# Decay attention and a hard-swish MLP on one core: the first batch's maxima leave by GpSimd's queue, and the MLP's last products rotate over five PSUM buffers

## The chip, the cores and the metric

The kernel runs on one core of one Trainium2 chip. The metric is the time of one execution on the device in microseconds (us). Each kernel is run several times and the median counts. TensorE (PE) multiplies matrices into PSUM, VectorE (DVE), ScalarE (ACT) and GpSimd (POOL) work element by element, and SyncE (SP) issues transfers (DMAs). Each engine runs its instructions in the order in which they were laid down at build time and waits on semaphores for what the others have not finished. GpSimd can also issue transfers, in line with its own instructions.

## The reference

Eight batches of eight heads (576 positions, 64 wide) go through attention with a learned decay; the result, 4608 rows of 512, goes through a two-layer network with a hard-swish between the layers.

```python
scores = scale * np.matmul(q, k.transpose(0, 1, 3, 2))
cum = np.cumsum(np.log(np.clip(f, 0.0001, 1.0)), axis=-1)
decay = cum[:, :, :, None] - cum[:, :, None, :]
scores = np.where(causal, -1000000000.0, scores + decay)
scores = scores - np.max(scores, axis=-1, keepdims=True)
attn = np.exp(scores)
attn = attn / (np.sum(attn, axis=-1, keepdims=True) + 1e-09)
x = np.matmul(attn, v)           # then transposed to 4608 x 512
h = x @ w_in                     # 512 x 2048
g = h * np.clip(h + 3.0, 0.0, 6.0) / 6.0
out = g @ w_out                  # 2048 x 512
```

[...]

## The kernel before, in words

**The weights.** w_in and w_out come in 16 chunks each of 512 KB (`w_load`, the DMA on L238, by SP). Each chunk is decoded (ACT L251, DVE L252 and L253), squared and summed (ACT L257); per group of four chunks of w_in, and once for the whole of w_out, a scale is worked out (`pow2_scale`, a matmul on L184 and four small DVE steps; L341 for w_out), and each chunk is split into a high and a low half of 16 bits: ACT L284 writes the high one. For the first three groups of w_in the low one goes through PE (L287, L288, tiles `low`) and ACT L289; for the last group of w_in and all 16 chunks of w_out it is one DVE instruction of 128x512 (L295). The second layer's first product (`po`, L832) can start only once w_out is split.

**The first batch's attention.** Batch 0 is worked in 12 steps, which `VH` lists: four pairs of heads on their first 256 queries (kind A), then eight heads on the rest (kind B). Each step takes the maximum per query of a first, cheaper product: `natural` (PE L495, tile `pn`, then DVE L501 into `MC`), `max_rows` (PE L510 turns the maxima into rows, tile `ptm`; DVE L512 negates them into `mr`, of which there is one buffer; a DMA on L513 puts them into row 96 of `TQ`), and then `scores` (PE L559, L560, L562 into `ps`, which reads that row; ACT L578 takes the exponential) and `av` (PE L713). POOL copies queries and keys and takes the low halves (L449, L450, L464, L469). The other 56 heads (`rows`, kind F) take another path without L513.

**The MLP.** `h_unit` makes 128 of the 2048 hidden units for 512 rows (`ph`, PE L785 to L787, then ACT L791, DVE L794, ACT L795, DVE L796), `out_unit` a 128x512 block of the output (`po`, PE L832 to L834, ACT L838, the DMA on L841). `rest_unit` (`ph_r`, L808 to L810, then ACT L817, DVE L821, ACT L823, DVE L824) and `out_unit` again (`po_r`) do the 64 odd rows of two batches together. These units are spread between the steps of attention by a count of credits (`fill`).

**PSUM.** Eight banks: pool `ps_s` has two buffers of two banks each (`pn` and `ps` of attention), `ps_m` two of one bank, `ps_t` one, and `pav` takes the last. `mm_tile` gives each unit of the MLP its PSUM tile: by turns two of three from `ps_m` and the third from `ps_t`.

**What sets the order.** The program is written in one order, but at build time a scheduler simulates it and lays down each engine's instructions in the order in which it finds them ready. Where a queue or a pool changes, its order can change on all engines. One help ties a few loads by hand: `pinned()` sets that what is issued within it comes after the instruction last put into the list `small`, and acts between instructions of one engine. The list holds the DMAs of L430 (the decay rows, by SP) and those of L513, one more with each of the 12 steps. `pinned()` holds the first eight loads of w_in (L236) and all loads of the values V (L353), both on SP.

Of the kernel before, what the change touches and what calls it, by code (L numbers as in the profile page):

```python
# [11 lines left out]
F32 = mybir.dt.float32  # L12
# [8 lines left out]
def kernel(  # L21
# [10 lines left out]
    nc = tc.nc  # L32

    NHEAD, D, S = qk.shape
# [5 lines left out]
    P = 128  # L40
# [6 lines left out]
    TT = 512  # L47
# [7 lines left out]
    ps_s = ctx.enter_context(tc.tile_pool(name="ps_s", bufs=2, space=bass.MemoryType.PSUM))  # L55
# [52 lines left out]
    TQ = [cpool.tile([97, SP], F32R, name=f"TQ{i}") for i in range(NQK)]  # L108
# [365 lines left out]
    def chunks(v):  # L474
        kind = VH[v][0]
        if kind == "A":
            c = [(h * QA + i * P, h * QA, P, (i + 1) * P, 512 * h + P * i) for h in range(2) for i in range(CA)]
            return [list(enumerate(c)), []]
        places = {3: 0, 2: 512, 4: 384}
        return [  # L480
            [(c - CA, ((c - CA) * P, 0, CR[c], c * P + CR[c], places[c])) for c in h]
            for h in ((3, 2), (4, ))
        ]
# [22 lines left out]
    def max_rows(v):  # L506
        i = v % NQK
        m = sum(len(x) for x in chunks(v))
        pt = ps_t.tile([P, 512], F32, tag="tr", name=f"ptm_{v}")
        nc.tensor.matmul(pt[:m, :P], MC[v % 2][:, 0:m], identr, start=True, stop=True)  # L510
        mr = p2.tile([NCH, P], F32R, tag="mr", name=f"mr_{v}", bufs=1)
        nc.vector.tensor_scalar(mr[:m], pt[:m, :P], -1.0, None, op0=ALU.mult)  # L512
        d = nc.sync.dma_start(TQ[i].bitcast(F32)[96:97, 0:m * P], mr.bitcast(F32)[:m])  # L513
        small.append(d.ins)


# [233 lines left out]
    def x_move(v):  # L750

        kind, n = VH[v]
        g = n if kind == "A" else n // 2
        b, cc = divmod(g, NPAIR)
        xhl = xpair[g][1]
        c0, c1, rest = {"A": (0, CA, None), "B": (CA, NCH - 1, NCH - 1), "F": (1, NCH, 0)}[kind]
        o = c0 - (1 if kind == "F" else 0)
        if rest is not None:
            nc.sync.dma_start_transpose(
                xT[2][:, cc, b // 2, :, 64 * (b % 2):64 * (b % 2) + 64],  # L760
                xhl[0:64, rest].rearrange("p a e -> p (a e)"),
            )
        nc.sync.dma_start_transpose(
            xT[b % 2][:, cc, o:o + c1 - c0].rearrange("p c a t -> p (c a) t"),
            xhl[:, c0:c1].rearrange("p c a e -> p (c a e)"),
        )


    turn = [0]

    def mm_tile(name, three):

        turn[0] += 1
        if three and turn[0] % 3 == 0:
            return ps_t.tile([P, TT], F32, tag="tr", name=name)
        return ps_m.tile([P, TT], F32, tag="mm", name=name)

    def h_unit(x, fc, c0, c1, b, three, name):

        nw = c1 - c0  # L780
        ph = mm_tile(f"ph_{name}_{fc}_{c0}", three)[:, :nw]
        fs_ = slice(fc * P, (fc + 1) * P)
        for cc in range(NCC):
            xh, xl = (x[:, cc, c0 // P:c1 // P, hl] for hl in range(2))
            nc.tensor.matmul(ph, w1[0][:, cc, fs_], xh, start=(cc == 0), stop=False)  # L785
            nc.tensor.matmul(ph, w1[0][:, cc, fs_], xl, start=False, stop=False)  # L786
            nc.tensor.matmul(ph, w1[1][:, cc, fs_], xh, start=False, stop=(cc == NCC - 1))  # L787
            if cc == 1 and nw == TT:
                yield H_COST
        r = p2.tile([P, TT], F32, tag="rt", name=f"r_{name}_{fc}_{c0}", bufs=3)[:, :nw]  # L790
        nc.scalar.activation(  # L791
            r, ph, AF.Relu, bias=bias_r, scale=scol(A1 + NG * b + fc * NG // NFC)
        )
        nc.vector.scalar_tensor_tensor(r, r, 6.0 * CG, ph, op0=ALU.min, op1=ALU.mult)  # L794
        nc.scalar.copy(gT[:, 0, fc, c0:c1], r)  # L795
        nc.vector.tensor_tensor(gT[:, 1, fc, c0:c1], r, gT[:, 0, fc, c0:c1], op=ALU.subtract)  # L796
        yield H_COST
# [47 lines left out]
    def moe_in(b, c0=0, c1=TT):  # L845

        for fc in range(NFC):
            j, new = divmod(fc, NFC // NG)
            if new == 0 and c0 == 0:
                while j not in w_in_done:  # L850
                    next(w_in_q, None)
                moe_scale_in(b, j)
            yield from h_unit(xT[b % 2], fc, c0, c1, b, b > 0 or c0 > 0, f"{b}")

    def moe_out(b, c0=0, c1=TT):

        if b == 0:
            for _ in wq:
                pass
        if c0 == 0:  # L860
            moe_scale_out(b)
        for s in range(c0 // P, c1 // P):
            r = S * b + (64 if b else 0) + s * P
            yield from out_unit(s, UO + b, [(r, r + P)], b > 0 or s * P >= QA, f"{b}")
# [4 lines left out]
    def rest_in(k, g):  # L869

        for j in range(NG):
            yield from rest_unit(k, j, g)

    def rest_out(k, g):

        b = 2 * k
        r = S - 64 if b == 0 else S * b
        yield from out_unit(
            0, UX + b + 1, [(r, r + 64), (S * (b + 1), S * (b + 1) + 64)], True, f"r{k}", g
        )  # L880
# [30 lines left out]
    for i in range(NL):  # L911
        nc.gpsimd.memset(T1[i].bitcast(F32)[:, S:], 0.0)
    max_rows(0)
    rests(0)
    load_x(2)
# [17 lines left out]
    def fill(k):  # L933
        credit[0] += k * rates[0]
        while credit[0] >= 1 and units:
            with tc.high_priority(offset=-LOW_M):
                r = next(units[0], 0)
            if r == 0:
                units.pop(0)
            else:  # L940
                credit[0] -= r
        credit[0] = min(credit[0], 1.0)

    def done(v):
        kind, n = VH[v]
        if kind == "A":
            if n == NPAIR - 1:
                units.append(moe_in(0, 0, QA))
                units.append(moe_out(0, 0, QA))
            return  # L950
        b, h = divmod(n, H)
        if h == H - 1:
            cut = QA if b == 0 else 0
            units.append(moe_in(b, cut, TT))
            if b == B - 1:
                units.append(rest_in(b // 2, g_end))
            units.append(moe_out(b, cut, TT))
            if b == B - 1:
                units.append(rest_out(b // 2, g_end))
            elif b % 2:  # L960
                units.append(rest_in(b // 2, gT))
                units.append(rest_out(b // 2, gT))

    prev = None
    pend_x = None
    vq = v_scale(0)
    for i, (kind, n) in enumerate(VH):
# [27 lines left out]
        if i + 1 < NV and VH[i + 1][0] != "F":  # L995
            max_rows(i + 1)
# [32 lines left out]
        prev = (i, ph)  # L1029
# [2 lines left out]
    fill(4)  # L1032
    x_move(prev[0])
    done(prev[0])
    while units:
        fill(1)

# [35 lines left out]
```

## Time and profile before

| | before |
|---|---|
| median of 3 runs | 1069.62 us (1068.02 to 1071.15) |
| profiled execution | 1067.75 us |
| its span, first to last instruction | 1065.7 us |
| PE busy | 1005.6 us (94%) |
| DVE busy | 714.6 us (67%) |
| ACT busy | 633.5 us (59%) |
| POOL busy | 439.4 us (41%) |
| mean granted TensorE clock | 0.988 of full speed |

The span is the time from the first to the last instruction of the profiled execution; its own time on the device is 2.05 us longer. The views give, per line of the program, how long an engine was busy, how long it idled before those instructions, and whose work ended the idling. "L295 DVE ... w<-w,SC" is line 295 on VectorE, output and inputs by the program's names. A table by stages gives each engine's busy time, and in brackets its instructions, within one stretch of the span.

### The profile page before, as it was taken

Reading aid. Unit: us, or ns where it says so; the run is one execution under the profiler, and the core shown is the slowest. Engines: PE = TensorE matmul, PEld = TensorE weight load, DVE = VectorE, ACT = ScalarE, POOL = GpSimd, SP = SyncE. Lnnn points to the kernel's source line nnn. Section 1 sums busy time; section 2 is a strip of 40 time slices with the busy share of each in tenths; the row PEclk is TensorE's granted clock in tenths of the full one; section 3 lists DMA queues with packets and bytes.
Section 4 is the critical chain, followed back from the end, with each engine's and each line's share of the span. In section 5 each row is a group of like instructions: output and inputs, shape, how many; then the busy total and the mean of one; then the engine's idle time right before and its main releaser. Section 6 shows DMA issues by size and latency. Waiting matters only on the chain.

```text
span 1065.7 us, 21332 instructions
## 1 busy us (share of the span) xinstructions
PE 1005.6 (94%) x7650; PEld 598.6 (56%) x7650; DVE 714.6 (67%) x1887; ACT 633.5 (59%) x1257; POOL 439.4 (41%) x641
## 2 busy tenths in 40 slices
PE   2799967899999999999999999999999999999897
PEld 2567844665555755555555755555555755444543
DVE  6878799886867678866885778847895677115300
ACT  5798667766864657656755657646764666125301
POOL 9635556435544445454553445545544430000000
PEclk9999989999999999999999999999999999999999
DMA  8875446936766675567565755566556544010000
GB/s 239 275 216 174 110 101 136 210 77 118 158 118 120 119 160 106 95 144 154 104 125 109 160 112 109 106 130 163 105 97 137 91 89 74 12 40 1 1 20 30
DMA packets 253717, 123.83 MB, mean 116 GB/s; under 512 B 225860, under 2 KB 227452, under 8 KB 253612
## 3 DMA queue, kind: packets, MB, share of 16 engines
q1 hardware_dynamic: 253612, 122.47, 53.2%
q8 instruction: 60, 0.98, 0.4%
q14 instruction: 45, 0.37, 0.1%
HBM read 47.93 MB, written 9.73 MB: 54 GB/s over the span
## 4 chain that ended last, share of the span: by engine, by line
PE 81%; DVE 9%; ACT 4%; DMA 4%; issue 2%; SPq 0%; POOL 0%; ACTq 0%; DVEq 0%; POOLq 0%
PE ph L785 10%; PE ph L786 10%; PE ph L787 10%; PE po L832 10%; PE po L834 10%; PE po L833 10%; PE pn L622 3%; PE pn L619 3%; DMA ring<-in_w_in_dram 2%; DVE pp L630 1%; PE pav L706 1%; PE pav L707 1%; PE pav L705 1%; PE po_r L834 1%; PE ph_r L808 1%
## 5 line engine op out<-in xcount | busy, mean ns | idle before, releaser
L642 ACT ACTIVATE pp<-pp,nb 128x192 f32<-128x192 f32 x280 | 138.4, 552 | 133.7 <-DVE nb L636 119.6
L785 PE MATMUL ph<-xT,w 128*128 128x512 f16 (+1 forms) x576 | 198.4, 358 | 3.6 <-ACT o L838 2.3
L659 DVE TENSOR_TENSOR ring<-pp,ring 128x128 f16<-128x128 f32 (+2 forms) x216 | 142.2, 671 | 83.5 <-ACT ring L656 77.8
L787 PE MATMUL ph<-xT,w 128*128 128x512 f16 (+1 forms) x576 | 197.9, 357 | 0.0
L786 PE MATMUL ph<-xT,w 128*128 128x512 f16 (+1 forms) x576 | 197.8, 357 | 0.0
L832 PE MATMUL po<-w,gT 128*128 128x512 f16 x512 | 189.5, 381 | 7.5 <-ACT w L284 3.5
L833 PE MATMUL po<-w,gT 128*128 128x512 f16 x512 | 192.1, 381 | 3.7 <-DVE w L295 3.7
L464 POOL TENSOR_TENSOR T<-ST,TQ 64x288 fp32r<-64x288 f32 (+2 forms) x136 | 112.0, 825 | 199.2 <-PE pn L622 153.0
L834 PE MATMUL po<-w,gT 128*128 128x512 f16 x512 | 191.7, 381 | 0.0
L630 DVE CUSTOM_DVE_ANT_0 pp<-pn,W 128x192 f32<-128x192 f32 x280 | 123.5, 483 | 32.1 <-PE pn L622 21.9
L794 DVE SCALAR_TENSOR_TENSOR r<-r,ph 128x512 f32<-128x512 f32 (+1 forms) x144 | 89.1, 620 | 68.1 <-ACT r L791 67.5
L619 PE MATMUL pn<-TK,TQ 68*128 68x192 f32 x336 | 125.9, 388 | 5.8 <-issue 5.7
L469 POOL TENSOR_TENSOR T<-ST,T 64x288 fp32r<-64x288 f32 (+1 forms) x136 | 125.5, 941 | 12.6 <-ACT T L462 7.9
L791 ACT ACTIVATE r<-ph,bias_r,SC 128x512 f32<-128x512 f32 (+1 forms) x144 | 103.8, 725 | 26.0 <-PE ph L787 22.8
L796 DVE TENSOR_TENSOR gT<-r,gT 128x512 f16<-128x512 f32 (+1 forms) x144 | 102.5, 714 | 23.5 <-ACT gT L795 21.8
L622 PE MATMUL pn<-T,T 128*128 128x192 f32 x336 | 116.0, 370 | 0.0
L656 ACT CAST ring<-pp 128x192 f16<-128x192 f32 x280 | 114.4, 450 | 0.2
L795 ACT CAST gT<-r 128x512 f16<-128x512 f32 (+1 forms) x144 | 81.1, 566 | 40.6 <-DVE r L794 40.2
L665 POOL TENSOR_TENSOR ring<-pp,ring 128x128 f16<-128x128 f32 x96 | 56.1, 584 | 104.0 <-ACT ring L656 84.4
L834 PEld LDWEIGHTS <-gT 128*128 128x128 f16 x560 | 54.7, 98 | 70.0 <-issue 10.3
L833 PEld LDWEIGHTS <-gT 128*128 128x128 f16 x560 | 54.9, 98 | 65.1 <-issue 10.2
L787 PEld LDWEIGHTS <-w 128*128 128x128 f16 x576 | 56.5, 98 | 57.0 <-issue 6.6
(159 smaller groups left out, 2036.3 us busy)
## 6 DMA issues: line engine op xcount, KB each, us to landing
ST<-in_qk_dram SPq DMA_DIRECT2D x64, 288.0 KB
ring<-in_w_out_dram SPq DMA_DIRECT2D x16, 512.0 KB
out_dram<-o SPq DMA_DIRECT2D x32, 256.0 KB
T<-TQ SPq DMA_DIRECT2D x56, 144.0 KB
vst<-in_vS_dram SPq DMA_DIRECT2D x7, 1040.0 KB
ring<-in_w_in_dram SPq DMA_DIRECT2D x9, 512.0 KB
w<-in_w_in_dram SPq DMA_DIRECT2D x7, 512.0 KB
vst<-in_vS_dram SPq DMA_DIRECT2D x14, 130.0 KB
```

What stands on the lines that cost most here:

```text
L469: nc.gpsimd.tensor_tensor(T1[j][0:D, a:e], s[D:, a:e], T1[j][D:, a:e].bitcast(F32), op=ALU.subtract)
L619: nc.tensor.matmul(dst, TQ[i][0:D + 4, qs], TK[i][0:D + 4, a:e], start=True, stop=False)
L622: nc.tensor.matmul(dst, T7[j][:, qs], T1[j][:, a:e], start=False, stop=True)
L630: nc.vector.tensor_tensor_reduce(pp[:r, w:w + kw], pn[:r, o:o + kw], W[:r, 4 * P + r - kw:4 * P + r], 1.0, -3.0e38, ALU.add, ALU.max, accu ...
L642: nc.scalar.activation(x_, x_, AF.Exp, bias=nb[:r, e0 + x:e0 + x + 1], scale=0.125)
L659: eng.tensor_tensor(hl[:r, a:a + c * P], pp[:r, at[c] + 64:at[c] + kw], hl[:r, h0[c] + 64:h0[c] + kw], op=ALU.subtract,)
L785: nc.tensor.matmul(ph, w1[0][:, cc, fs_], xh, start=(cc == 0), stop=False)
L786: nc.tensor.matmul(ph, w1[0][:, cc, fs_], xl, start=False, stop=False)
L787: nc.tensor.matmul(ph, w1[1][:, cc, fs_], xh, start=False, stop=(cc == NCC - 1))
L832: nc.tensor.matmul(po, g[:, 0, fc, ts_], w2[:, fc, 0, :], start=(fc == 0), stop=False)
L833: nc.tensor.matmul(po, g[:, 0, fc, ts_], w2[:, fc, 1, :], start=False, stop=False)
L834: nc.tensor.matmul(po, g[:, 1, fc, ts_], w2[:, fc, 0, :], start=False, stop=(fc == NFC - 1))
```

## The change

The DMA of L513, twelve times, is issued by POOL in place of SP. It is still put into `small`, so the list now holds POOL's instructions, and the loads in `pinned()` are on SP. After the last head's outputs have been moved, a list `heads_done` is no longer empty, and from then on `mm_tile` takes each odd turn from `ps_s`, whose two buffers attention no longer uses (512 of their 1024 columns); even turns go on as before.

```diff
@@ max_rows
         mr = p2.tile([NCH, P], F32R, tag="mr", name=f"mr_{v}", bufs=1)
         nc.vector.tensor_scalar(mr[:m], pt[:m, :P], -1.0, None, op0=ALU.mult)
-        d = nc.sync.dma_start(TQ[i].bitcast(F32)[96:97, 0:m * P], mr.bitcast(F32)[:m])
+        d = nc.gpsimd.dma_start(TQ[i].bitcast(F32)[96:97, 0:m * P], mr.bitcast(F32)[:m])
         small.append(d.ins)
@@ mm_tile
     turn = [0]
+    heads_done = []
 
     def mm_tile(name, three):
 
         turn[0] += 1
+        if heads_done and turn[0] % 2:
+            return ps_s.tile([P, 1024], F32, tag="S", name=name)[:, :TT]
         if three and turn[0] % 3 == 0:
             return ps_t.tile([P, TT], F32, tag="tr", name=name)
         return ps_m.tile([P, TT], F32, tag="mm", name=name)
@@ the end of the program
     fill(4)
     x_move(prev[0])
     done(prev[0])
+    heads_done.append(prev[0])
     while units:
         fill(1)
```

Lines below 770 stand three further down in the changed kernel (L832 becomes L835). The scheduler lays the work down in another order in two stretches: from the start up to the end of w_out's split, and after the last head. Between them, and in what is executed, nothing differs on PE, DVE and ACT. The following shows three of the places, each row an instruction with its line, its output and inputs, and their shape; the numbers in the names tell buffers apart.

SP's queue near the start, from the first rows of the decay on. `TK<-cs` are the decay rows of the first two pairs of heads, `T_101<-TQ_93` the queries' halves of the first, and `w_115`, `ring` the slots for chunks of w_in. Before:

```order
L409 DMA ST_104<-in_qk_dram 128x2x256
L409 DMA ST_105<-in_qk_dram 128x2x256
L430 DMA TK_96<-cs 2x1x256 x2
L430 DMA TK_97<-cs 2x1x256 x2
L461 DMA T_101<-TQ_93 64x512
L917 DMA decay_dram<-cs 64x1152
L238 DMA ring_125<-in_w_in_dram 128x1024
L238 DMA w_115<-in_w_in_dram 128x1024
L424 DMA TK_98<-decay_dram 2x2x256
L409 DMA ST_103<-in_qk_dram 128x2x256
L513 DMA TQ_93<-mr_186 1x4x128
L355 DMA v_111<-in_vS_dram 128x3x520
```

and in the changed kernel:

```order
L409 DMA ST_104<-in_qk_dram 128x2x256
L409 DMA ST_105<-in_qk_dram 128x2x256
L355 DMA v_111<-in_vS_dram 128x3x520
L356 DMA xT_118<-in_vS_dram 128x520
L357 DMA xT_118<-in_vS_dram 64x520
L238 DMA w_115<-in_w_in_dram 128x1024 x2
L430 DMA TK_96<-cs 2x1x256 x2
L430 DMA TK_97<-cs 2x1x256 x2
L461 DMA T_101<-TQ_93 64x512
L920 DMA decay_dram<-cs 64x1152
L238 DMA ring_123<-in_w_in_dram 128x1024
L238 DMA ring_125<-in_w_in_dram 128x1024
```

The three loads of V and two chunks of w_in have moved ahead of the first pairs' decay rows, and L513 is gone from the queue. On PE the same start has the `low` products of the first chunks of w_in ahead of the first pair's scores; in the changed kernel these rows stand just ahead of and at the first `ps`, which before follows the second `pn` at once:

```order
L288 MATMUL low_343<-w_113,ident_80 128x512
L510 MATMUL ptm_247<-identr,MC_107 4x128
L287 MATMUL low_348<-gT,eye_296 128x512
L288 LDWEIGHTS ident_80
L288 MATMUL low_348<-w_113,ident_80 128x512
L184 MATMUL pt_w_440<-wm_390,ones 128x1
L287 MATMUL low_450<-gT,eye_447 128x512
L287 MATMUL low_455<-gT,eye_447 128x512
L288 LDWEIGHTS ident_80
L288 MATMUL low_455<-w_113,ident_80 128x512
L288 LDWEIGHTS ident_80
L288 MATMUL low_450<-w_113,ident_80 128x512
```

Six `low` products and the scale of w_in's second group thus come before the first pair's scores; in the kernel before, all of them come after the second pair's.

DVE's queue where w_out's split begins, from the scale (L341) on; L659, L665 and L670 are work of F heads, L400 the split of V for them. Before:

```order
L389 COPY SC<-SC 64x1
L295 SCALAR_TENSOR_TENSOR w_115<-w_115,SC 128x512
L659 TENSOR_TENSOR ring_123<-pp_0_1680,ring_123 128x128
L400 SCALAR_TENSOR_TENSOR v_111<-vst,SC,v_111 128x5x64 x6
L659 TENSOR_TENSOR ring_123<-pp_0_1680,ring_123 128x512
L665 TENSOR_TENSOR ring_123<-pp_0_1680,ring_123 128x2x64
L670 TENSOR_TENSOR ring_123<-pp_0_1680,ring_123 64x64
```

and in the changed kernel:

```order
L341 TENSOR_SCALAR SC<-SC 128x4
L386 TENSOR_TENSOR SC<-SC 128x1
L512 TENSOR_SCALAR mr_1512<-ptm_1510 3x128
L739 RECIPROCAL rs_0_1473<-rs_0_1473 128x3
L388 COPY SC<-SC 64x1
L740 TENSOR_TENSOR xf_1471<-pav,rs_0_1473 128x3x64
L295 SCALAR_TENSOR_TENSOR w_115<-w_115,SC 128x512 x3
L734 TENSOR_SCALAR rs_1_1560<-pav,SC 128x3
L739 RECIPROCAL rs_1_1560<-rs_1_1560 128x3
L740 TENSOR_TENSOR xf_1471<-pav,rs_1_1560 128x3x64
L295 SCALAR_TENSOR_TENSOR w_115<-w_115,SC 128x512
```

The scale of w_out stands earlier against the heads: the last B head's L512, which before stands 37 rows ahead of L341, now comes behind it. From L341 to the last of the 16 L295 DVE's queue has 137 rows before, with the maxima (L630) of five F heads between, and 101 rows with those of three in the changed kernel. The matmul of w_out's scale (L184) is PE's row 726 before and 672 now.

PE's queue near the end: `ph_r_3` is the last group of hidden units of the odd rows, `po_r_0` the last block of the output. Before:

```order
L833 MATMUL po_r_0_12595<-w_115,vst 128x512
L834 LDWEIGHTS vst
L834 MATMUL po_r_0_12595<-w_115,vst 128x512
L808 LDWEIGHTS w_113
L808 MATMUL ph_r_3_12328<-xT_119,w_113 128x128
L809 LDWEIGHTS w_113
L809 MATMUL ph_r_3_12328<-xT_119,w_113 128x128
L810 LDWEIGHTS w_114
L810 MATMUL ph_r_3_12328<-xT_119,w_114 128x128
L832 LDWEIGHTS vst
L832 MATMUL po_r_0_12595<-w_115,vst 128x512
```

and in the changed kernel:

```order
L813 MATMUL ph_r_3_12328<-xT_119,w_114 128x128
L813 LDWEIGHTS w_114
L813 MATMUL ph_r_2_12273<-xT_119,w_114 128x128
L835 LDWEIGHTS gT
L835 MATMUL po_3_12543<-w_115,gT 128x512
L836 LDWEIGHTS gT
L836 MATMUL po_3_12543<-w_115,gT 128x512
L837 LDWEIGHTS gT
L837 MATMUL po_3_12543<-w_115,gT 128x512
```

Before, 36 of the 48 `po_r` products stand ahead of the last three of `ph_r_3`, and 12 behind them. In the changed kernel all of `ph_r` is done some 96 products before the end, and `po_3` and then `po_r` follow it.

## The prediction

> **What bounds the kernel now.** I read the table by stages first, then PE's waits in the stages where PE idles, then the rows around them. Columns of the first table: start and end of the stage, its length, then the busy time (and in brackets the instructions) of PE, PE's weight loads, DVE, ACT and POOL, the granted clock, the DMA share and GB/s.
>
> ```profile
> 0.00:37.00 37.00, 14.68 (x59) 12.36 (x60) 26.07 (x76) 19.56 (x38) 28.84 (x49) 1.00 0.86 262
> 37.00:100.00 63.00, 54.62 (x337) 40.09 (x336) 53.04 (x168) 57.50 (x120) 32.93 (x39) 0.95 0.74 218
> ...
> 140.00:200.00 60.00, 42.89 (x355) 26.77 (x354) 57.61 (x146) 43.99 (x91) 38.13 (x46) 0.90 0.71 148
> 200.00:340.00 140.00, 139.51 (x1130) 85.11 (x1128) 103.86 (x300) 92.37 (x194) 62.82 (x92) 1.00 0.65 129
> 340.00:900.00 560.00, 559.05 (x4561) 323.40 (x4560) 409.20 (x1055) 353.70 (x704) 253.46 (x383) 1.00 0.60 119
> 900.00:1066.00 166.00, 154.85 (x885) 75.73 (x883) 33.44 (x51) 39.54 (x61) 0.00 (x0) 0.99 0.05 17
> ```
>
> From 200 to 900 us PE is busy for all but 1.4 us of 700, and the change moves nothing in most of it: PE bounds it. PE idles 22.3 us up to 37, 8.4 up to 100, 17.1 from 140 to 200, and 11.2 after 900, of 60 in all. Only there can a new order gain, and the PE work itself (1005.6 us) stays. In the third of these stages DVE is busy for 57.6 of 60 us, so there it is DVE that sets the pace. What PE waits for in it, and below it what it waits for in the last 76 us (us in total, times, the longest):
>
> ```profile
> PE pn L619 <- issue: 5.7, 2, 3.6
> PE po L833 <- DVE w L295: 3.7, 5, 1.1
> PE po L832 <- ACT w L284: 3.5, 1, 3.5
> PE ph L785 <- ACT o L838: 2.3, 1, 2.3
> ```
>
> ```profile
> PE po L832 <- DVE r_r L821: 2.7, 1, 2.7
> PE po_r L832 <- ACT vst L823: 2.5, 1, 2.5
> ```
>
> Two of the first four rows name the split of w_out, on which the second layer's first product rests. The other list is the tail: twice PE has nothing to do while ACT and DVE make hidden units.
>
> **Part one, the tail (five PSUM buffers).** The rows of the end:
>
> ```profile
> 1001.95 0.38 PE L832 MATMUL po<-w,gT 128*128 128x512 f16 x1 [2.75 <-DVE r_r L821]
> ...
> 1051.08 0.38 PE L832 MATMUL po_r<-w,vst 128*128 128x512 f16 x1
> 1051.29 0.38 PE L833 MATMUL po_r<-w,vst 128*128 128x512 f16 x1
> ...
> 1053.78 0.22 PE L810 MATMUL ph_r<-xT,w 128*128 128x128 f16 x1
> 1054.04 1.02 ACT L817 ACTIVATE r_r<-ph_r,bias_r,SC 128x256 f32<-128x256 f32 x2 [8.58 <-PE ph_r L810]
> ...
> 1056.48 0.39 PE L832 MATMUL po_r<-w,vst 128*128 128x512 f16 x1 [2.49 <-ACT vst L823]
> ...
> 1060.35 0.63 PE L834 MATMUL po_r<-w,vst 128*128 128x512 f16 x1
> 1061.02 0.69 ACT L838 ACTIVATE o_r<-po_r,SC 128x512 f32<-128x512 f32 x1 [4.59 <-PE po_r L834]
> ```
>
> With three buffers a tile comes back after three turns, so a new `po` waits until `ph_r`'s has been read (2.75 us). The last `ph_r_3` products stand behind 36 `po_r` products, and the chain L817, L821, L823 after them has nothing on PE beside it: 2.49 us. The 12 products left then ran from 1056.48 to the read at 1061.02, 4.5 us; the same products just before start 0.21 us apart (1051.08, 1051.29), 12 of which make 2.6: they lose 1.9 after the pause. Together 2.75 + 2.49 + 1.9 = 7.1 us. In the changed order `ph_r_3` is done 96 products before the end, 96 x 0.215 = 20.6 us of cover for a chain of about 2.5 us, and a tile comes back after four turns or more. What is late next is the last output's own path (L838 and its DMA, as before). Bounds: only the last pause goes, 2.49; or all of it and the rest of the stage's idling, 11.2 less the 5 us that follow PE's end, some 6 to 7.1 as well, so 2.5 to 7.9. I take 6.2: nearly all, less something for the first turns, in which even turns still share three buffers.
>
> **Part two, w_out's split.** The scale is found at L341, then 16 L295 follow, among the heads' work:
>
> ```profile
> 136.76 0.71 DVE L341 TENSOR_SCALAR SC<-SC 128x4 f32<-128x4 f32 x1
> 140.66 0.75 DVE L295 SCALAR_TENSOR_TENSOR w<-w,SC 128x512 f16<-128x512 f32 x1
> 192.96 0.75 DVE L295 SCALAR_TENSOR_TENSOR w<-w,SC 128x512 f16<-128x512 f32 x1
> ```
>
> ```profile
> L295 DVE SCALAR_TENSOR_TENSOR w<-w,SC 128x512 f16<-128x512 f32 x16 | 14.3, 894 | 0.4 <-ACT w L284 0.3
> ```
>
> The 16 take 14.3 us of DVE, but from L341 to the last of them 56.2 us pass, since five F heads stand between: 137 rows of DVE. The new order has 101 rows there, with three heads. In proportion that is 56.2 x 101 / 137 = 41.4 us, 14.8 less. PE's idling shrinks at best by those 14.8, and at least in proportion to the stretch, 17.1 x 14.8 / 56.2 = 4.5. I take the middle, 9.5. The heads that are put off need DVE later, but from 200 to 340 us DVE has 36.1 us free, over twice 14.8; were that cover gone, PE would wait there for `pp`. Bounds: 0 (the pause only moves) and 17.1 (all of it).
>
> **Part three, the start.** Here the queue matters. The first row is PE's first product and then each stage's first scores; the SP rows are issues of L513:
>
> ```profile
> 12.63 1.22 PE L495 MATMUL pn<-TK,TQ 66*128 66x128 f32 x4 [12.63 <-POOL TQ L450]
> 21.40 0.58 PE L559 MATMUL ps<-TQ,TK 97*128 97x256 f32 x1 [1.13 <-DMA TQ<-mr]
> 40.79 0.39 PE L559 MATMUL ps<-TQ,TK 97*128 97x256 f32 x1 [0.17 <-DMA TQ<-mr]
> 53.96 0.61 PE L559 MATMUL ps<-TQ,TK 97*128 97x320 f32 x1 [1.45 <-DMA TQ<-mr]
> ...
> 78.97 1.02 PE L287 MATMUL low<-gT,eye 128*128 128x512 f32 x2
> 80.19 1.02 PE L287 MATMUL low<-gT,eye 128*128 128x512 f32 x2
> ```
>
> ```profile
> 18.14 0.68 SPq L513 DMA_DIRECT2D TQ<-mr  x1
> 33.44 0.62 SPq L513 DMA_DIRECT2D TQ<-mr  x1
> ```
>
> ```profile
> w<-in_w_in_dram SPq DMA_DIRECT2D x7, 512.0 KB
> v<-in_vS_dram SPq DMA_DIRECT2D x1, 780.0 KB
> xT<-in_vS_dram SPq DMA_DIRECT2D x1, 260.0 KB
> xT<-in_vS_dram SPq DMA_DIRECT2D x1, 130.0 KB
> ```
>
> The trace has no transfer by POOL. By SP one took from issue to the scores 3.3 us (18.14 to 21.40) alone and 7.3 (33.44 to 40.79) among loads; only its issue cost 0.68. So I put a POOL transfer between 0.7 and 7.3 us, at 3.3, by the nearest row: no change on the path. The Trainium skill, "DMA: Bandwidth & Descriptors", in its section on the anatomy of a DMA by GpSimd's path, gives 2.0 us plus bytes / 436e3, so about 2.0 us for these 1.5 to 2 KB as an estimate; no row here shows it, and by it the sum would be the same within 1.3 us a step. POOL's queue is in order too, and it waits for PE:
>
> ```profile
> POOL T L464 <- PE ps L560: 29.7, 7, 6.5
> ```
>
> So from the third step on L513 stands behind an L464 that waits for an earlier step's scores (29.7 us in seven waits up to 120 us). That is the old dependence of step on step, not a new one, as long as the scores come in time.
>
> What moves more is the loads. Their pin acts on SP alone, and its anchor is now on POOL. V's three loads (780 + 260 + 130 KB) and two chunks (1024 KB) come ahead of the decay rows of the first pair: 2.25 MB at the 262 GB/s of that stage are 8.6 us, so the first `pn` goes from 12.6 to about 21. Its scores then also stand behind six `low` products, which need decoded chunks; before, such products start at 35.7 and the fourth ends at 44.7. I put the first `ps` at 37, between the plain shift (21.4 + 8.6 = 30) and 44: 15.6 us later. What comes back: all 12 `low` are done ahead of the fifth step, where before it is four of them: 8 x 1.22 (80.19 less 78.97) = 9.8 us off the later stretch. And the chunks come earlier, so that ACT waits less for them:
>
> ```profile
> ACT gT L251 <- DMA ring<-in_w_in_dram: 9.3, 5, 3.8
> ACT gT L251 <- DMA w<-in_w_in_dram: 2.2, 3, 1.2
> ```
>
> Half of these 11.5 us are 5.8. So 15.6 - 9.8 - 5.8 = 0. Bounds: +15.6, nothing back; and 8.6 - 9.8 - 11.5 = -12.7.
>
> **The sum.** 1067.75 - 6.2 - 9.5 + 0 = 1052.05 on the profiled execution; the median of the runs is 1.87 above that one, so 1053.9, say 1054 us.
>
> **The rivals.**
>
> *The start loses for good* (slower). The first scores come 15.6 us late, the twelve steps run one behind the other as before (each needs the one before through POOL's L464 and the single `mr`), and the F heads behind them are as late, so that w_out's split loses the same cover. For it: POOL's 29.7 us of waits for scores show how tight the steps are chained. Against it: `low` and decoding are needed anyway. Price: 1069.62 - 6.2 + 15.6 = 1079. It decides from the point at which the start's loss exceeds what the split gives by more than 9.4 us (6.2 and 3.2).
>
> *Only the tail is gained.* What the split gains the start loses: 1069.62 - 6.2 = 1063. For it: both come from one shift of heads against weights.
>
> *All three gain.* The first stages have 30.7 us of PE idling; with chunks in time some 8 of them go as well: 1046.
>
> *The edit does nothing in the tail, or little, and the start cancels:* 1069. Against it: the pause of 2.49 us has no cause but the order of the rows, which has changed.
>
> *DVE holds up POOL's transfers.* DVE is busy for 53.0 of 63 us in the stage of most steps; if POOL's issue waits out one DVE instruction each time, by the row
>
> ```profile
> L794 DVE SCALAR_TENSOR_TENSOR r<-r,ph 128x512 f32<-128x512 f32 (+1 forms) x144 | 89.1, 620 | 68.1 <-ACT r L791 67.5
> ```
>
> that is 12 x 0.62 = 7.4 us, and the time 1061. The Trainium skill, "SBUF — State Buffer", has this as a trap under "Who interferes with whom": POOL writes the descriptors of its own transfers and is locked out while DVE runs certain two-port instructions, 620 ns alone against 3100 under a copy. By these figures it would be an estimated 30 us for all twelve; no run here has shown it yet.
>
> **Chances.** Forecast 0.43; only the tail 0.17; all three 0.15; the start loses for good 0.11; nothing 0.08; DVE holds up the transfers 0.06. About 0.3%, 3.2 us, is what a measurement of this kernel can tell from no change. Faster: 0.43 + 0.15 + 0.06 and nearly all of 0.17, 0.79. Same: the 0.08 and an edge of the tail's case, 0.10. Slower: 0.11. The range takes in the forecast's own bounds, the tail's case and the lower one: 1044 to 1067; the slower case, no change and what of "all three" falls lower stay out, about 0.2.
>
> **What would show it.** In the stage from 140 to 200 us (or where `po` first starts) PE's idling should fall from 17.1 to about 8, with the stretch from L341 to the last L295 near 41 us. The first `pn` should start near 21 and the first `ps` near 37; if that `ps` comes and the first F head is later by as much, the slower rival holds. PE's waits for `TQ<-mr` should stay within 3 us in all; more than 6 speaks for DVE's hold. In the tail the pauses of 2.75 and 2.49 us should both be gone and the last `po_r` products 0.21 us apart; if one remains with another releaser, part one is too large. I am wrong altogether if PE idles more than 60 us in all.

## The result, and the profile after

The changed kernel takes 1063.99 us (median of 20 runs, 1060.19 to 1070.46) against 1069.98 us for the kernel before (20 runs, 1066.68 to 1072.15). The ratio is 0.9947, with a 95% interval of 0.9933 to 0.9960: 5.7 us faster, where 15.6 were forecast. The sign was right and the time lies in the range, but the gain is little over a third of what the sum gave.

The profiled execution of the changed kernel took 1070.46 us (span 1068.5), the longest of the 20 and 6.5 us more than their median. Its stages are therefore read for where time goes, and the sizes are checked on the experiments. The table by stages of the changed kernel (columns as in the prediction):

```profile
0.00:37.00 37.00, 13.85 (x30) 6.83 (x31) 26.56 (x76) 23.99 (x49) 22.75 (x40) 0.97 0.94 294
37.00:100.00 63.00, 50.56 (x241) 37.52 (x240) 47.50 (x138) 46.46 (x95) 34.40 (x44) 0.72 0.65 205
100.00:134.00 34.00, 34.00 (x262) 29.11 (x262) 22.82 (x62) 21.51 (x46) 13.81 (x23) 0.90 0.21 56
...
140.00:200.00 60.00, 54.09 (x406) 36.70 (x404) 55.55 (x149) 42.94 (x83) 38.20 (x47) 1.00 0.46 104
200.00:340.00 140.00, 135.26 (x1136) 84.52 (x1135) 116.04 (x324) 96.33 (x203) 71.90 (x102) 0.98 0.74 146
340.00:900.00 560.00, 559.25 (x4565) 323.76 (x4564) 407.37 (x1064) 352.45 (x705) 258.00 (x390) 1.00 0.60 120
900.00:1069.00 169.00, 163.68 (x970) 81.16 (x968) 42.44 (x71) 46.55 (x76) 1.63 (x3) 0.99 0.09 23
```

Two columns tell it. PE's idling from 140 to 200 us is 5.9 us in place of 17.1. And the granted clock from 37 to 100 us is 0.72 in place of 0.95. To put both in one unit I cut the span into windows of 1 us and took PE's busy time in each times what the clock lacks of 1 as time lost by the clock. It is an approximation, but over all kernels below the two together foretell within 5 us how much later a fixed piece of later work starts (products that a kernel adds counted in).

| stage, us | PE idle / lost by the clock, before | changed kernel | difference |
|---|---|---|---|
| 0 to 37 | 22.3 / 0.0 | 23.1 / 0.7 | +1.5 |
| 37 to 140 | 8.4 / 2.3 | 12.4 / 19.2 | +21.0 |
| 140 to 200 | 17.1 / 4.5 | 5.9 / 0.0 | -15.7 |
| 200 to 340 | 0.5 / 0.6 | 4.7 / 3.2 | +6.8 |

Worked out from unrounded values, that is 13.6 us more up to 340 us. The fixed piece is the 17th F head's first product, behind which PE's order is the same in both kernels up to the tail (the last row that stands elsewhere is at 306 us in the changed kernel). Before:

```profile
338.69 0.44 PE L619 MATMUL pn<-TK,TQ 68*128 68x192 f32 x1
```

and in the changed kernel:

```profile
349.83 0.44 PE L619 MATMUL pn<-TK,TQ 68*128 68x192 f32 x1
```

It starts 11.1 us later, but the span ends only 2.8 us later, so the tail has gained 8.3 us. The end of the changed kernel's timeline:

```profile
1063.08 0.38 PE L836 MATMUL po_r<-w,vst 128*128 128x512 f16 x1
1063.30 0.38 PE L837 MATMUL po_r<-w,vst 128*128 128x512 f16 x1
1063.71 0.69 ACT L841 ACTIVATE o_r<-po_r,SC 128x512 f32<-128x512 f32 x1 [3.41 <-PE po_r L837]
1064.43 1.12 SPq L844 DMA_DIRECT2D out_dram<-o_r  x2
```

The products stand 0.22 us apart up to the last, and the list of PE's waits after 890 us is empty: the pauses of 2.75 and 2.49 us and the slow last twelve are gone.

### The profile page after: what moved, and what is told of

It is laid out like the page before. It is cut to its first block, busy times and chain, and to the rows that moved or that the text cites. A ratio compares the mean times of both kernels' runs of the same rounds, so it can differ in the third digit from the quotient of the medians.

```text
span 1068.5 us, 21314 instructions
## 1 busy us (share of the span) xinstructions
PE 1016.7 (95%) x7650; PEld 605.0 (57%) x7650; DVE 721.1 (67%) x1887; ACT 634.3 (59%) x1257; POOL 445.4 (42%) x653
## 4 chain that ended last, share of the span: by engine, by line
PE 79%; DVE 9%; ACT 4%; DMA 4%; issue 3%; POOL 1%; SPq 0%; ACTq 0%; DVEq 0%; POOLq 0%
PE po L835 9%; PE po L836 9%; PE po L837 9%; PE ph L788 9%; PE ph L789 9%; PE ph L790 9%; PE pn L622 3%; PE pn L619 3%; PE pav L713 3%; DVE pp L630 2%; DMA w<-in_w_in_dram 2%; PE ph_r L811 1%; PE ph_r L812 1%; PE ph_r L813 1%; PE po_r L835 1%
## 5 line engine op out<-in xcount | busy, mean ns | idle before, releaser
L659 DVE TENSOR_TENSOR ring<-pp,ring 128x128 f16<-128x128 f32 (+2 forms) x216 | 138.8, 657 | 84.4 <-ACT ring L656 80.5
L835 PE MATMUL po<-w,gT 128*128 128x512 f16 x512 | 189.9, 380 | 0.6 <-ACT w L284 0.4
L630 DVE CUSTOM_DVE_ANT_0 pp<-pn,W 128x192 f32<-128x192 f32 x280 | 123.6, 483 | 29.7 <-PE pn L622 19.2
L799 DVE TENSOR_TENSOR gT<-r,gT 128x512 f16<-128x512 f32 (+1 forms) x144 | 105.1, 735 | 19.3 <-ACT gT L798 17.5
L665 POOL TENSOR_TENSOR ring<-pp,ring 128x128 f16<-128x128 f32 x96 | 57.3, 596 | 111.1 <-ACT ring L656 88.0
```

The costliest lines, as they stand in the source:

```text
L630: nc.vector.tensor_tensor_reduce(pp[:r, w:w + kw], pn[:r, o:o + kw], W[:r, 4 * P + r - kw:4 * P + r], 1.0, -3.0e38, ALU.add, ALU.max, accu ...
L659: eng.tensor_tensor(hl[:r, a:a + c * P], pp[:r, at[c] + 64:at[c] + kw], hl[:r, h0[c] + 64:h0[c] + kw], op=ALU.subtract,)
L835: nc.tensor.matmul(po, g[:, 0, fc, ts_], w2[:, fc, 0, :], start=(fc == 0), stop=False)
```

## The experiments

Two theories went in. **A**: the tail's gain is PSUM's alone; the start loses by the loads that lost their pin, not by POOL's queue, and what it loses is mostly the half clock that follows PE's idle stretches. **B**, the rival: POOL's queue itself costs (its place in line, or DVE holding it up), and the clock is a bystander. All kernels were timed against the kernel before on the same chip; the last two columns come from the one profiled execution of each.

| kernel | median, us | ratio to before, 95% interval | 17th F head, us | from there to the end, us |
|---|---|---|---|---|
| before | 1068.7 to 1070.0 | | 338.7 | 727.0 |
| changed, first comparison | 1063.99 | 0.9947 (0.9933 to 0.9960) | 349.8 | 718.7 |
| changed, again | 1064.71 | 0.9968 (0.9951 to 0.9986) | 348.0 | 718.7 |
| PSUM part alone | 1061.00 | 0.9922 (0.9908 to 0.9936) | 341.1 | 718.0 |
| PSUM part alone, again | 1061.15 | 0.9932 (0.9912 to 0.9953) | 339.1 | 718.7 |
| queue alone | 1073.62 | 1.0044 (1.0026 to 1.0063) | 342.8 | 728.9 |
| on SP, nothing pinned | 1073.75 | 1.0038 (1.0021 to 1.0056) | 341.1 | 724.8 |
| on POOL, pinned to L461 | 1080.65 | 1.0096 (1.0071 to 1.0120) | 355.3 | 725.7 |
| queue alone, 54 products more | 1076.95 | 1.0074 (1.0055 to 1.0092) | 346.0 | 727.4 |
| before, 54 products more | 1075.84 | 1.0057 (1.0038 to 1.0077) | 346.7 | 728.2 |
| PSUM part, V not pinned | 1074.75 | 1.0052 (1.0033 to 1.0070) | 353.1 | 718.6 |
| PSUM part, w_in not pinned | 1079.84 | 1.0096 (1.0073 to 1.0118) | 356.7 | 718.8 |
| changed, 18 products more | 1081.19 | 1.0118 (1.0093 to 1.0142) | 360.4 | 718.9 |
| PSUM part, half the low halves on POOL | 1085.90 | 1.0161 (1.0135 to 1.0187) | 366.6 | 718.2 |
| changed, 15 products more, order kept | 1062.04 | 0.9932 (0.9908 to 0.9956) | 341.9 | 718.8 |
| changed, 19 products more | 1062.40 | 0.9935 (0.9917 to 0.9952) | 340.9 | 718.3 |
| PSUM part, 7 products more | 1060.59 | 0.9924 (0.9904 to 0.9944) | 338.4 | 718.8 |

### The two parts apart

The PSUM part alone:

```diff
+        if heads_done and turn[0] % 2:
+            return ps_s.tile([P, 1024], F32, tag="S", name=name)[:, :TT]
...
+    heads_done.append(prev[0])
```

> The PSUM part alone, L513 on SP as before. Theory A (the tail's gain is all of PSUM's making and the start's is lost by the order of loads): 6 to 8 us faster than before, 1062 to 1064, all of it after the last head, with PE idle for about 5 us after 900 us in place of 11; the stages up to 340 us as before. Rival (the tail's gain needs the shifted heads): within 3 us of before.

Measured: 1061.00 us, 7.8 us faster than before. That is within the 6 to 8 us expected; the time itself lies 1 us below the range, since the kernel before took 1068.8 beside it. PE's order is that of the kernel before, row for row, up to some 900 us. Run again beside the changed kernel:

> 1060 to 1062.5, as in the first run of it, and faster than the changed kernel by 2 to 5 us; from the 17th F head to the end 718 to 719 us as in the changed kernel.

1061.15 us, as expected, and 3.6 us faster than the changed kernel beside it. The last column of the table settles the tail: from the 17th F head to the end the six profiles with three buffers took 724.8 to 728.9 us, the eleven with five 718.0 to 718.9, whatever happened ahead of it.

The queue alone:

```diff
-        d = nc.sync.dma_start(TQ[i].bitcast(F32)[96:97, 0:m * P], mr.bitcast(F32)[:m])
+        d = nc.gpsimd.dma_start(TQ[i].bitcast(F32)[96:97, 0:m * P], mr.bitcast(F32)[:m])
```

> The queue of L513 alone, three PSUM buffers at the end. Theory A: 0 to 4 us slower than before, 1070 to 1074: from 140 to 200 us PE idles about 11 us less, and the start loses as much again, about 5 us by idling and the rest by a granted clock of half in several stretches between 30 and 110 us. Rival (the queue's part gains as well and the tail gave back): 1060 to 1066.

Measured: 1073.62 us, 4.8 us slower than before, 0.8 more than A allowed. Its stages from 37 us on:

```profile
37.00:100.00 63.00, 52.59 (x261) 40.11 (x261) 50.95 (x143) 49.15 (x100) 37.11 (x50) 0.71 0.67 215
100.00:140.00 40.00, 39.64 (x323) 33.82 (x320) 26.81 (x83) 24.83 (x50) 15.82 (x26) 0.98 0.18 47
140.00:200.00 60.00, 53.17 (x432) 36.47 (x431) 55.54 (x146) 44.09 (x89) 39.58 (x49) 1.00 0.54 116
200.00:340.00 140.00, 135.65 (x1115) 82.34 (x1115) 117.15 (x319) 96.66 (x203) 75.80 (x106) 1.00 0.71 145
```

The pattern is the changed kernel's: 6.8 us of idling from 140 to 200 us, but a clock of 0.71 from 37 to 100. The changed kernel itself, beside the PSUM part alone:

> The changed kernel itself, beside the PSUM part alone on the same chip. By the runs so far 1062 to 1066, some 3 us slower than the PSUM part alone, if the two parts simply add (the queue alone cost 4.8 us); if they help each other, no slower than it.

1064.71 us. A gain of 7.8 and a loss of 4.8 make 3.0; the two comparisons of the changed kernel gave 5.7 and 3.4 (by the ratios). The parts add, within what the intervals allow.

### The queue or the loads

L513 stays on SP, and what it puts into the list holds nothing:

```diff
     def pinned():
-        return tc.issue_after(small[-1]) if small else nullcontext()
+        return tc.issue_after(small[-1]) if small and small[-1] is not None else nullcontext()
...
-        small.append(d.ins)
+        small.append(None)
```

> L513 stays on SP, but nothing is pinned to it any more, so that SP's queue starts with the same loads in the same places as in the changed kernel; PSUM as before. Theory A (the order of loads does it, not the queue): within 3 us of the kernel with the queue alone, first scores at 37 to 41 us, first F head near 150. Rival B (POOL's queue or DVE's hold on it costs): at or below the kernel before, 1060 to 1068, since only the gain from 140 to 200 us is left.

Measured: 1073.75 us, a ratio of 1.0038 against the queue alone's 1.0044, with first scores at 37.05 us (36.86 there). B expected 1068 or less. So the loss is there without POOL's queue, once the loads come in the new order. The two kernels are not the same otherwise: SP issues the loads alike up to 30 us, but PE's order differs from 50 to 299 us, so the equal times alone don't show that the queue is free. The changed kernel's own transfers say more. The first two rows give KB each and the median us from issue to landing, the third is an issue in the timeline of POOL:

```profile
TQ<-mr POOLq DMA_DIRECT2D x8, 1.5 KB, 1.9
TQ<-mr POOLq DMA_DIRECT2D x4, 2.0 KB, 3.6
```

```profile
85.60 0.59 POOL L513 DMA_DIRECT2D TQ<-mr  x1 [1.82 <-DVE rs L739]
```

They landed in 1.9 and 3.6 us by the median (the longest, the first, took 6.7), an issue took 0.59 us, and among PE's waits up to 340 us there is none for `TQ<-mr` any more. No cost of POOL's queue shows.

Then the loads pinned again, with L513 on POOL:

```diff
-        nc.sync.dma_start(T7[j].bitcast(F32)[0:D, 0:nq], TQ[i].bitcast(F32)[0:D, 0:nq])
+        d = nc.sync.dma_start(T7[j].bitcast(F32)[0:D, 0:nq], TQ[i].bitcast(F32)[0:D, 0:nq])
+        if VH[v][0] != "F":
+            small.append(d.ins)
```

> L513 on POOL, and the loads pinned again, to SP's own L461 of each step; PSUM as before. Theory A: within 3 us of before, 1067 to 1073, with the first scores near 21 to 26 us and the granted clock up to 134 us as before. Rival B (POOL's queue costs by itself): 4 us or more slower than before, PE waiting for the maxima's transfers for more than 6 us in all.

It took 1080.65 us, 11.9 us slower than before: A's forecast failed. B's time came, but not its sign: PE waited for the maxima's transfers for 2.5 us in all, not for more than 6. But the order was not restored either. L461 comes earlier than L513, V's loads stood right behind the first one, the first scores came at 31.7 us (21.4 before), PE idled 15.2 us from 140 to 200 us and 7.7 from there to 340. It is therefore no clean test of the queue; it shows that a third order of the same loads is worse than both.

Which loads matter was asked with five PSUM buffers and L513 on SP, once with V's loads free and once with w_in's:

```diff
-    PIN_V = 1
+    PIN_V = 0
```

> L513 on SP, five PSUM buffers, V's loads not pinned and w_in's pinned as before. If V's loads ahead of the first decay rows are what costs: 4 us or more slower than the PSUM part alone, 1065 or above. If the early chunks of w_in do it (theory A): within 3 us of the PSUM part alone, 1058 to 1064, with the first low products near 36 us and PE's idling from 140 to 200 us near 17.

```diff
-        with pinned() if PIN or i == 0 and k < 8 else nullcontext():
+        with pinned() if PIN or i == 0 and k < 0 else nullcontext():
```

> L513 on SP, five PSUM buffers, w_in's loads not pinned and V's pinned as before. Theory A (the early chunks bring both the gain from 140 to 200 us and the start's loss): 2 to 6 us slower than the PSUM part alone, 1063 to 1067, PE idling from 140 to 200 us below 10. If V's loads are what costs: faster than the PSUM part alone by 4 us or more, 1057 or below.

They came out 13.8 and 18.8 us slower than the PSUM part alone, where both sets freed together (the queue alone) cost 4.8. The first fits the words of its V branch, 4 us or more slower. The second fits neither branch, and under V's it should have been faster, so the two together fit neither theory. With V free the first scores came at 30.1 us and PE lost 15.9 us by the clock from 37 to 100; with w_in free PE idled 29.4 us up to 37 and 16.6 from 140 to 200. The loss cannot be divided among the loads: each change makes the scheduler lay down another order on PE up to some 300 us, and what was measured is that order as a whole.

### The crunch at w_out's split

```diff
-    POOL_REST = ((0, 0, 0, 0), (0, 0, 0, 0))
+    POOL_REST = ((0, 0, 0, 0), (0, 1, 0, 1))
```

> The PSUM part alone, and every second low half of w_out made by POOL in place of DVE (eight instructions, 7.2 us of DVE between 136 and 200 us less, eight more on ACT); PE's order is the same up to w_out's scale. If DVE's load sets the pace there (step two of the prediction): PE idles 4 to 10 us less than 17 from 140 to 200 us, and the kernel takes 1053 to 1059. If the place of the split among the heads does: the split ends later (seven heads' maxima between in place of five), and the kernel is no faster, 1060 to 1066.

1085.90 us, slower than either branch expected. DVE was busy for 52.3 us of that stage, 6 less than in the PSUM part alone, but PE idled 19.1 us there and 14.1 us from 200 to 340. So less work on DVE did not shorten the stage here, and with seven heads' maxima among the split it got longer. That fits the prediction's proportion, which went by how the split stands among the heads, and it gives no support to its sentence that DVE sets the pace there. But PE's order changed as well, and how much of the loss is POOL's share of the split (1.2 us for a low half, 0.8 on DVE), this run does not tell.

### Does the half clock cost the time?

First, six products of 128x512 ahead of the first scores of nine steps, whose results are overwritten, in the kernel with the queue alone and in the kernel before:

```diff
+            if pc == 0 and 1 <= v <= 9:
+                for _ in range(6):
+                    nc.tensor.matmul(ps[:, 0, :], ident16, W[:, 0:512], start=True, stop=True)
```

> The kernel with the queue alone, and ahead of the first scores of nine steps six products of 128x512 more, whose result is overwritten: 54 in all, 11.6 us of PE at full clock, put where PE waits for a step. Theory A (the start's loss is the half clock that follows PE's idle stretches): the loss by a clock below 1 between 37 and 140 us falls from about 17 us to below 8, so that the kernel is at most 2 us slower than the queue alone, and relative to it does better than the same products do to the kernel before by 5 us or more. Rival (PE merely waits, and the clock is a bystander): 5 to 12 us slower than the queue alone, 1079 to 1086.

> The kernel before with the same 54 products. It loses only 2 to 5 us to the clock in the start, so there is little to win: Theory A: 3 to 9 us slower than before, 1072 to 1078. Rival: the same 5 to 12 us as in the changed start.

The loss by the clock from 37 to 140 us fell from 16.7 to 4.8 us in the first. It became 3.3 us slower than the queue alone; the kernel before became 7.2 us slower by the same products. The difference, 3.9 us (2.9 by the ratios), has A's sign but not its size, and 3.3 is more than the 2 that A allowed and less than the rival's 5 to 12. The build had also moved other rows, as it did with two products for each step in the changed kernel:

> The changed kernel with two products of 128x512 more ahead of the first scores of nine steps, 18 in all, 3.9 us of PE at full clock. If the half clock after idle stretches is what the start loses (theory A): a mean clock of 0.985 or more and a time no longer than the changed kernel's, 1060 to 1065. Rival (PE is only given more to do): 2 to 4 us slower than the changed kernel.

That one took 1081.19 us, 16.5 more than the changed kernel, for 3.9 us of work: its order differs up to 340 us, with 10.7 and 8.6 us of idling in the last two stages in place of 6.3 and 5.5. Neither theory speaks to it. Added work tests the clock only where the order stays.

So the next kernels add products only at places that leave the order of the other rows on PE as it was: eleven into the tile of the maxima ahead of L510 of five steps, two ahead of a `pn`, one each ahead of two `low` products. One line of it:

```diff
-        pt = ps_t.tile([P, 512], F32, tag="tr", name=f"ptm_{v}")
+        pt = ps_t.tile([P, 512], F32, tag="tr", name=f"ptm_{v}"); [nc.tensor.matmul(pt, ident16, W[:, 0:512], start=True, stop=True) for _ in range({4: 4, 5: 3, 1: 2, 6: 1, 11: 1}.get(v, 0))]
```

> The changed kernel with 15 products of 128x512 more (3.2 us of PE at full clock) at places of the start where the order of everything else on PE stays what it is, row for row; their results are overwritten. Theory A (the start loses by the half clock that follows idle stretches, and dense products end it): the loss by the clock from 37 to 140 us falls from about 20 us to 14 or less, and the kernel is no slower than the changed one in spite of 3.2 us more of work: 1058 to 1064. Rival (the clock is a bystander): 2 to 6 us slower than the changed kernel, 1066 to 1070.

Measured: 1062.04 us, ratio 0.9932. With 15 products more the kernel is not slower than the changed one (0.9947 and 0.9968); by the middle of the ratios it is 1.6 to 3.8 us faster, with overlapping intervals. The loss by the clock from 37 to 140 fell from 19.2 and 20.7 us (the two profiles of the changed kernel) to 12.6. PE's rows are the changed kernel's, row for row, with 15 put in between. One caution: PE's idling up to 340 us is 2.4 us less than in the changed kernel, so most of the 3.2 us of new work fell where PE stood idle, and by the rival's own reasoning the kernel need only have been about 1 us slower. And with 19: ten at such places ahead of other work, and nine of 128x384, two behind the sixth step's L510 and seven behind the seventh's, near the idle stretch before 87 us:

```diff
-        nc.tensor.matmul(pt[:m, :P], MC[v % 2][:, 0:m], identr, start=True, stop=True)
+        nc.tensor.matmul(pt[:m, :P], MC[v % 2][:, 0:m], identr, start=True, stop=True); [nc.tensor.matmul(pt[:, 128:512], ident16, W[:, 0:384], start=True, stop=True) for _ in range({5: 2, 6: 7}.get(v, 0))]
```

> The changed kernel with 19 such products, seven of them (of 128x384) in the idle stretch before 87 us after which the half clock lasts 20 us; the order of the rest differs in 147 rows between 82 and 125 us and nowhere else. Theory A: the half clock from 86 to 107 us goes or is cut to below 10 us, a mean clock of 0.986 or more, and 1056 to 1062. Rival: 2 to 6 us slower than the changed kernel, 1066 to 1070.

1062.40 us, ratio 0.9935, and 7.8 us lost by the clock. The table by stages around that place, first of the changed kernel:

```profile
62.00:73.00 11.00, 10.54 (x43) 8.13 (x44) 7.22 (x28) 8.00 (x17) 4.63 (x7) 0.53 0.56 157
73.00:84.00 11.00, 8.26 (x49) 7.05 (x48) 10.81 (x31) 8.22 (x19) 8.97 (x7) 0.84 0.52 165
84.00:87.00 3.00, 0.00 (x0) 0.00 (x0) 1.67 (x8) 1.38 (x3) 1.24 (x3) 0.87 0.74 161
87.00:106.00 19.00, 18.63 (x83) 15.22 (x83) 11.54 (x26) 11.56 (x24) 8.28 (x13) 0.50 0.69 224
```

and of the kernel with 19 products more:

```profile
62.00:73.00 11.00, 8.89 (x63) 6.87 (x63) 10.59 (x39) 9.90 (x19) 5.12 (x8) 1.00 0.71 221
73.00:84.00 11.00, 7.66 (x31) 5.44 (x31) 9.19 (x25) 7.44 (x18) 6.55 (x7) 0.62 0.60 169
84.00:87.00 3.00, 3.00 (x18) 2.51 (x17) 0.26 (x1) 0.96 (x2) 0.00 (x0) 0.67 0.96 378
87.00:106.00 19.00, 16.99 (x139) 14.34 (x139) 17.73 (x43) 15.91 (x36) 11.10 (x16) 1.00 0.55 167
```

In the changed kernel PE stands still from 84 to 87 us and then works almost without a pause for 19 us at a clock of 0.50: 83 products. With the filling, the same 19 us hold 139 products at full clock. Here the order is not wholly kept: of the rows that move, one pair stands between 87 and 104 us, the others behind it, up to 134 us. The 17th F head starts at 340.9 us in place of 348.0 and 349.8, but those two executions of the changed kernel took 3.9 and 6.5 us more than their medians, so most of that lead is theirs. B's 2 to 6 us more did not come; the first time lies within A's bounds, the second 0.4 us above them. The kernel with 15 products carries the verdict, since there the order is kept: work was added, the loss by the clock fell, and the kernel did not get slower. That it got faster, by some 2 us, is at the edge of what these intervals can tell.

In the PSUM part alone, whose start is that of the kernel before, the same filling with seven products of 128x384 has less to win:

> The PSUM part alone with seven products of 128x384 (1.1 us) behind the maxima of the fifth and seventh step, all else on PE in the same order. Its half clock from 51 to 62 us stands behind an idle stretch of 3 us there. Theory A: that stretch is shortened and the kernel takes 1057 to 1061, 0 to 4 us less than the PSUM part alone. Rival: 1061 to 1063.

1060.59 us, ratio 0.9924 against 0.9922 and 0.9932: inside A's bounds, and no difference that can be told. It and the PSUM part alone are the fastest kernels of this study, though the two filled changed kernels lie within 2 us of them, which the intervals can't tell apart. The PSUM part alone beat the changed kernel by 3.6 us in the direct comparison.

## Why the prediction came out as it did

**Part one, the tail: right, a little small.** 6.2 us were taken, 7.1 had been read off the three pauses, and 8.3 is what the two profiles show, 0.4 above the upper bound. All three losses went, and the reserve for the first turns was not needed. The remaining 1.2 us over the three terms are less than the spread of the tails with three buffers (724.8 to 728.9 us), and I did not follow them up.

**Part two, w_out's split: the stage was right, the cover half.** The changed kernel's stretch from the scale to the last L295:

```profile
142.41 0.27 DVE L341 TENSOR_SCALAR SC<-SC 128x4 f32<-128x4 f32 x1
188.21 0.74 DVE L295 SCALAR_TENSOR_TENSOR w<-w,SC 128x512 f16<-128x512 f32 x1
```

45.8 us in place of 56.2 (41.4 forecast). PE's idling fell by 11.2 us and the clock stayed up, which saved 4.5 more: 15.7, against 9.5 in the sum. But from 200 to 340 us, where I had named DVE's 36 free us as the cover, 6.8 us came back (3.2 in the queue alone). It is not untouched ground either: PE's order differs up to 306 us, and not only to the end of the split, as the section on the change has it. The net, 9 to 12 us, is close to the term, in part by luck: the 4.5 us of clock and what came back were both not in the sum.

**Part three, the start: this is the step that failed.** The sum said 15.6 us later, 9.8 and 5.8 coming back, so 0. The rows of the changed kernel, the first and the twelfth step's first scores and one of PE's waits between:

```profile
39.00 0.47 PE L559 MATMUL ps<-TQ,TK 97*128 97x256 f32 x1
...
148.41 0.41 PE L559 MATMUL ps<-TQ,TK 97*128 97x320 f32 x1
```

```profile
87.37 0.58 PE L788 MATMUL ph<-xT,w 128*128 128x256 f16 x2 [3.49 <-DMA xT<-xhl]
```

The first scores came at 39.0 us, as forecast (37), 17.6 us later than before, and the last `low` product started at 65.0 in place of 80.2. What did not arrive is the repayment. From the first step's scores to the twelfth's, the changed kernel took 109.4 us (39.0 to 148.4), the kernel before 104.8 (21.4 to 126.2), though six `low` products fewer stand in between. PE ran at half clock for much of it: 18.5 of these 109.4 us are lost to the clock, 2.3 of the 104.8. At full clock, by this estimate, the stretch would have been some 12 us shorter than before, against the 15.6 forecast: work was saved, and the half clock ate it. ACT's waits for chunks of w_in fell as well, from 11.5 to 7.4 us, where 5.8 us had been counted. The start's term was 0; up to 140 us it measured +18.1 us in the profiled execution of the queue alone, which is its median, and +22.5 in the long one of the changed kernel. Of these, 14.4 and 17.6 are clock, 3.6 and 4.9 idling. I had read the column of the clock in the table by stages, 0.95 and 1.00, and taken it as a constant, though the tail's third term was itself a loss after a pause (the granted clock from 1057 to 1061 us in the kernel before is 0.62).

What is shown is that the half clock costs the time there: the filled kernels take 7 to 13 of some 20 us of it away and are not slower for 3 to 4 us more of work. The row at 87.37 ends one of the pauses in which a half clock began (at 86.2 us): 3.49 us of waiting for `xT`, which in the changed order PE meets early. That it was the pauses that began it in each case is argued from their place, not shown. The runs' times go with their clock as well: among the changed kernel's 20 runs, which all have the same order and the same work, a line through time and mean clock falls by 0.6 us for each 0.001 of clock (correlation -0.78), from 1070.46 us at 0.975 to 1060.19 at 0.987.

**The rivals.** "Only the tail is gained" gave 1063 us at a chance of 0.17, and that is the time that came, for the reason it named: the start took what the split gave. That it fits to 1 us is luck, since the tail gave 2 us more than its 6.2 and the rest lost as much. "The start loses for good" was half right. By the sign given for it, a first F head later by as much as the first scores, it held: that head starts at 157.2 us in place of 132.1, which is even more. But w_out's split gained all the same. Neither "all three gain" nor "nothing" came. "DVE holds up POOL's transfers" has nothing for it: they landed in 1.9 and 3.6 us (medians), with DVE busy for 47.5 of the 63 us from 37 to 100. The trap that the Trainium skill describes in "SBUF — State Buffer", under "Who interferes with whom", did not show in this kernel.

**Still open:** what begins the half clock in each case and what keeps it up while PE is busy; and why V's or w_in's loads freed alone cost three to four times what both freed together cost. For the second, the profiles show where (idling and clock up to 340 us), but the order is the scheduler's, and no rule for it came out of these runs.

## What to carry to other kernels

Before counting moved work as repaid, look where the new order leaves the tensor engine idle for a few us among short products, and price the granted clock behind it: up to 340 us the queue alone saved 2.8 us of PE's idling and lost 9.3 us more by the clock. A change of queue can undo an ordering that hangs on that queue, so ask what is tied to the instruction that moves. Take the parts of an edit separately: the PSUM part alone was faster than the two together.

## What was not expected of the hardware

The half clock can last while PE is busy. In the kernel before it came once up to 140 us and ended after 7 us:

```profile
51.00:58.00 7.00, 4.78 (x20) 4.33 (x21) 5.51 (x16) 6.80 (x14) 2.15 (x3) 0.51 0.88 244
58.00:65.00 7.00, 7.00 (x36) 4.33 (x35) 5.90 (x22) 6.71 (x16) 4.37 (x6) 1.00 0.80 189
```

In the changed kernel it lasted from 87 to 106 us with PE busy for 18.63 of 19 us, and for all 19 in its second profile. The products bear the clock out: those of 128x256 start 0.21 us apart up to 106.5 us (105.39, 105.61, 105.82) and 0.11 apart behind it (106.80, 106.91). In all these traces the stretches at half clock of the start last 3.4, 6.8, 10.2 us or a higher multiple of 3.4, up to 27.3 in the queue alone. The Trainium skill, "TensorE: Matmul & The Clock Gate", Part 1, says that about 3.4 us of sustained work bring the full clock back. The first rows agree: PE is busy without a pause from 54.0 us on, and the full clock is back at 57.8. The 19 us do not agree with it, and here the measurement stands. In those 19 us many products are narrow, for example:

```profile
89.35 2.71 PE L713 MATMUL pav<-v,pf 128*128 128x96 f32 x12
99.75 2.87 PE L713 MATMUL pav<-v,pf 128*128 128x96 f32 x12
```

Whether such products count as too little work to lift the clock was not tried by itself, and one thing speaks against it: in the kernel before, the same kinds (scores, then twelve of 128x96) filled the 3.9 us from 54.0 to 57.8 in which the full clock came back. With seven products of 128x384 put ahead, the clock was full from 86 us on. With the 15 fillers, whose order is the changed kernel's, it still stood at 0.50 from 85 to 94 us while PE was busy all the time.
